# The start of a Fourier-mixing and gated feed-forward kernel, reordered: weight pieces first, then the input in thirds

## The chip, the cores and the metric

One core of a Trainium2 chip runs the whole program. The metric is the device time of one execution in microseconds (us); lower is better. TensorE (PE) multiplies matrices, VectorE (DVE), ScalarE (ACT) and GpSimd (POOL) do elementwise work, SyncE (SP) issues most of the transfers (DMA).

## The reference

```python
x: (8, 3008, 256) float32                       # batch, sequence, features
X = fft(fft(x, axis=1), axis=2).real            # Fourier mixing, real part
t = X.reshape(24064, 256)
gate = 1 / (1 + exp(-(t @ w_gate)))             # w_gate, w_val: (256, 1536)
val  = t @ w_val
out  = (gate * val) @ w_out                     # w_out: (1536, 256)
```

The three weights come as float64, so each stored word is two 32-bit halves, and the kernel makes float32 of them itself.

## The kernel before, in words

**Fourier part.** A sequence of one batch comes as four mirrored rows of slots (x4, 126 partitions, four parts h, six slots q, 256 features). The *fold* adds and subtracts the parts and the mirrored features, so that three kinds of columns are left: cosine columns (0), sine columns (1) and the lone middle feature E (2). PE multiplies them with a table of cosines and sines (`st`, loaded in pieces). The sums of even and odd slots (`ev`, `od`) are left in PSUM, ACT copies the first, DVE adds and subtracts the two (`places`, L509 and L512) into `pk` (cosine rows), `qk` (sine rows) and `ek` (E row). A closure `sums` issues the products of some slots, `then` the evacuation.

**Weights.** The feature transform is merged into the gate and value weights: a *piece* is 256 columns of a weight (512 KB as loaded). Two ACT activations (L297, L298), three DVE operations (L307, L308, L310) and one POOL addition (L312) make float32 of it: `weight_parts` and `weight_join`. `merge` then multiplies a gate or value piece with the table `dt` on PE, ACT copies the product into G1 and G2, and two small DMAs bring the row that belongs to E into `ge`, one column for each tile of features. There are 18 pieces: 6 gate, 6 value, 6 of w_out. A list `jobs` gives their order. For w_out no merge is done; `forms(g)` adds and subtracts its blocks into 15 forms (`wf`) for each of four groups g, on POOL for g = 0 and on DVE for the others.

**Steps.** For each batch the rows are cut into six chunks of 252 and each chunk has 12 tiles of features, so there are 576 steps i. A step has a first half (`front_a`: two products with G1 and pk, for gate and value), a second half (`front_b`: two with G2 and qk), the gates (`gate_a`, `gate_b`, one step later: two sigmoids on ACT, DVE operations z at L640, h at L652 and L654, and sums of h on POOL, L660, none, seven or six of them in three successive steps) and, from step 5 on, a third of `back`: five products that multiply the sums with `wf`, one group of three steps at a time. `back` of group p begins at step 3p + 5, and its first five products need all of `forms` of that group, since the fourth uses form 10, which is made last. The E term is *seeded* into PSUM from step 12 on: ACT writes E times `ge` (L600) before the products are added. In steps 0 to 4 PE adds it by two extra products, in steps 5 to 11 DVE does (L619).

**Order.** The program orders every engine by hand: what is issued first on an engine runs first, and an engine that waits holds all that is issued behind it. `pre` and `use` tell which pieces are converted or used in which step. Transfers on SP also share eight completion semaphores in turn (in the trace), so a later transfer is issued only when the one eight places earlier has landed.

**The start.** Pieces 0 and 1 are loaded, converted and merged, then x (two halves) is folded on DVE and POOL; cosine and E sums run, then the other pieces are converted between the evacuations, the sine sums wait for the second half of the table, and step 0 begins with pieces 2 and 3 still to be merged. The other ten gate and value merges and all forms run between the first steps.

Of the kernel before, what the change touches and what calls it, by code (L numbers as in the profile page):

```python
# [82 lines left out]
def kernel(  # L83
# [61 lines left out]
    def load_x(b):  # L145
        X[b] = xp.tile([P, 4, NQ, D], F32, name="x4", tag="x4")
        for h in range(0, 4, 2):
            if b:
                nc.sync.dma_start(out=X[b][:, h : h + 2], in_=XR[b][:, h : h + 2])
            else:  # L150
                nc.sync.dma_start(out=X[b][0:NP, h : h + 2], in_=xf[b, :, h : h + 2])
# [29 lines left out]
    G1 = const.tile([P, 2, F], F32, name="G1")  # L181
    G2 = const.tile([P, 2, F], F32, name="G2")
# [9 lines left out]
    def load_table(t, nq):  # L192
        for q in range(0, NQ, nq):
            yield nc.sync.dma_start(out=ST[0][0:NP, t, q : q + nq], in_=stab[:, t, q : q + nq])
# [14 lines left out]
    def table_odd():  # L209
# [21 lines left out]
        def tangent():  # L231
# [8 lines left out]
    jobs = [(0, 0), (1, 0), (0, 1), (1, 1), (2, 0), (0, 2), (1, 2), (2, 1), (0, 3), (1, 3), (0, 4), (2, 2),  # L240
            (1, 4), (0, 5), (1, 5), (2, 3), (2, 4), (2, 5)]
    RAW, WS = {}, {}
    shared = {}
    KEEP = 10

    def weight_load(j):
# [13 lines left out]
        def home(j):  # L260

            if j in (0, 1, 2, 3, 5):
                if j > 2:
                    ws = some(5, pqp, "qk")[:, (j // 5) * 2 * WC : (j // 5 + 1) * 2 * WC]
                    return sp.tile([P, 4 * WC], F32, name="raw", tag="sf"), ws
                t = hp.tile([P, 6 * WC], F32, name="raw", tag="h")
                return t[:, 0 : 4 * WC], t[:, 4 * WC :]
            if j in (4, 6, 9):
                t = wf[:, {4: 1, 6: 2, 9: 3}[j]].rearrange("p m n -> p (m n)")
                return t[:, 0 : 4 * WC], t[:, 4 * WC : 6 * WC]  # L270
            t = some(10, cp, "c")
            if j == 7:
                raw = pqp.tile([P, 4 * WC], F32, name="raw", tag="pk")
                return raw, t[:, 6 * WC : 8 * WC]
            return t[:, 0 : 4 * WC], t[:, 4 * WC : 6 * WC]

        if j < KEEP:
            raw, ws = home(j)
        else:
            both = some(24, xp, "x4").rearrange("p (i n) -> p i n", n=2 * WC)  # L280
            r, i = (j - KEEP) % 3 * 2, 6 + (j - KEEP) % 6
            raw, ws = both[:, r : r + 2].rearrange("p a n -> p (a n)"), both[:, i]
# [45 lines left out]

    def merge(ws, g, c, other):
        cs = slice(c * WC, (c + 1) * WC)  # L330
        ps = bank("ps", other)
        for h in range(2):
            for t in range(2):
                mm(ps[:, h * WC : (h + 1) * WC], dt[:, t, h * HD : (h + 1) * HD], ws[:, t, :],
                   h == 0 and t == 0, t == 1)
        nc.scalar.copy(G2[:, g, cs], ps[:, WC : 2 * WC])
        nc.scalar.copy(G1[:, g, cs], ps[:, 0:WC])
        for f in range(c * WC // P, (c + 1) * WC // P):
            (nc.sync if c else nc.scalar).dma_start(
                out=ge[:, g, f : f + 1], in_=G2[0:1, g, f * P : (f + 1) * P])  # L340

# [44 lines left out]
    def fold_ops(b, nq):  # L386
# [51 lines left out]
        else:  # L438

            def half1(q):  # L440
                point(nc.vector, 2, 3, q)
                first(nc.vector, 2, 3, q)
                for blk in range(2):
                    across(nc.vector, blk, q)
                    feat(nc.vector, *parts[blk], q)

            def half2(q):
                across(nc.vector, 0, q)
                feat(nc.vector, *parts[0], q)
                across(pool, 1, q)  # L450
                feat(pool, *parts[1], q)
            for q in qs:
                point(nc.vector, 0, 1, q)
            first(nc.vector, 0, 1, slice(0, NQ))
            point(pool, 2, 3, qs[1])
            first(pool, 2, 3, qs[1])
            ops += [lambda: half1(qs[0]), lambda: half2(qs[1])]
        for blk, (v, r) in enumerate(parts):
            if b and blk:
                W[b, blk] = v[:, :, HD:D], r[:, :, HD:D]  # L460
                continue
            W[b, blk] = (v[:, :, 0:HD], r[:, :, 0:HD],
                         v[:, :, HD : HD + 1].to_broadcast([v.shape[0], NQ, P]))
# [56 lines left out]
    def seq_start(b):  # L520
        PQE[b] = [pqp.tile([P, NK + 1], F32, name=name, tag=name) for name in ("pk", "qk")]
        if not b:
            PQE[b].append(op.tile([P, NK + 1], F32, name="ek", tag="os"))
# [5 lines left out]


# [60 lines left out]
    N1 = 5  # L591

    def seed(i):
# [5 lines left out]
        for g in range(2 if i >= NFT else 0):  # L599
            nc.scalar.activation(PF[i][:, g], EK[i // NFT], AF.Copy, scale=ge[:, g, f : f + 1])  # L600

    def front_a(i):
        (pk, *_), ks, _, _, fs = cut(i)
        if i < NFT:
            seed(i)
        for g in range(2):
            mm(PF[i][:, g], G1[:, g, fs], pk[:, ks], i < NFT and g == 0, True)
        for g in range(2 if i < N1 else 0):
            mm(PF[i][:, g], G2[:, g, fs], shared["qk"][:, 4 * WC : 4 * WC + CH], False, True)

    def part(i):
# [3 lines left out]
        if not N1 <= i < NFT:  # L615
            nc.scalar.activation(AP[i], PF[i], AF.Copy, scale=2.0)  # L616
            return
        for g in range(2):
            nc.vector.scalar_tensor_tensor(out=AP[i][:, g], in0=pqe[2][:, ks],  # L619
                                           scalar=ge[:, g, f : f + 1], in1=PF[i][:, g],  # L620
                                           op0=ALU.mult, op1=ALU.add)
# [6 lines left out]
    def gate_a(i):  # L628
# [7 lines left out]
        if N1 <= i < NFT:  # L636
            nc.vector.scalar_tensor_tensor(out=z[:, :, ::-1], in0=AP.pop(i), scalar=2.0, in1=PF[i],
                                           op0=ALU.mult, op1=ALU.subtract)
        else:
            nc.vector.tensor_tensor(z[:, :, ::-1], AP.pop(i), PF[i], op=ALU.subtract)  # L640
# [6 lines left out]
    def gate_b(i):  # L647
# [5 lines left out]
        nc.scalar.activation(pf[:, 0], z[:, 0], AF.Sigmoid)  # L653
        nc.vector.tensor_tensor(h[:, fh, n:], pf[:, 0], z[:, 1], op=ALU.mult)  # L654
# [145 lines left out]

    nc.gpsimd.memset(nil, 0.0)
# [3 lines left out]
    for j in range(2):  # L805
        weight_load(j)
    load_x(0)
    for _ in load_table(0, NQ // 2):
        pass
    for j in range(2, 5):  # L810
        weight_load(j)
    sines = load_table(1, NQ // 2)
    next(sines)
    for j in range(5, 7):
        weight_load(j)
    next(sines)
    for j in range(7, KEEP):
        weight_load(j)

    def weight_round(*js):  # L820
        for j in js:
            weight_parts(j)
            weight_join(j)

    weight_parts(0)
    weight_parts(1)
    weight_join(0)
    weight_join(1)
    weight_use(0)
    weight_use(1)  # L830
    seq_start(0)

    e0 = shared["qk"][:, 4 * WC : 4 * WC + CH]
    nc.gpsimd.memset(e0, 0.0)
    other = {(0, 0): (4, None), (0, 1): (4, None), (0, 2): (0, 1), (1, 2): (2, 3)}
    cos = [seq_group(0, blk, what, other.get((blk, what))) for blk in range(2) for what in (0, 2)]
    for i, f in enumerate(fold_ops(0, NQ // 2)):
        f()
        for sums, _, _ in cos:
            sums(*range(i * NQ // 2, (i + 1) * NQ // 2))  # L840
    sin = [seq_group(0, blk, 1, other.get((blk, 1))) for blk in range(2)]
    for i in range(2):
        for sums, _, _ in sin:
            sums(*range(i * NQ // 2, (i + 1) * NQ // 2))
    evacuate = [then for _, then, _ in cos + sin]
    for then, js in zip(evacuate, ((2, 3), (4,), (5,), (6,), (7,), (8,))):
        weight_round(*js)
        then()()
    nc.scalar.dma_start(out=ed[0:1], in_=PQE[0][2][0:1])
    nc.vector.tensor_copy(e0[0:1], PQE[0][2][0:1, 0:CH])  # L850
    weight_parts(9)
    for j in range(KEEP, KEEP + 3):
        weight_load(j)
    weight_use(2)
# [8 lines left out]
    pre, use = {}, {}  # L863
    for j, i in enumerate((0, 1, 2, 3, 4, 5, 6, 7, 9), 9):
        if i:
            pre.setdefault(i - 1, []).append(lambda j=j: weight_parts(j))
        pre.setdefault(i, []).insert(0, lambda j=j: weight_join(j))
        if KEEP <= j < len(jobs) - 3:
            at(i, lambda j=j: weight_load(j + 3))
    for j, i in enumerate((0, 0, 1, 2, 0, 3, 4, 5, 4, 6, 7, 8, 8, 8, 11), 3):  # L870
        use.setdefault(i, []).append(lambda j=j: weight_use(j))
    at(N1 - 1, lambda: nc.vector.tensor_copy(PQE[0][1][0:1, 0:CH], PQE[0][2][0:1, 0:CH]))
# [17 lines left out]
    for i in range(i0, count, i0):  # L890
        at(i - 8, lambda i=i: e_rows(i))
# [25 lines left out]
    for i in range(count):  # L917
        front_a(i)
        if N1 <= i < NFT:
            part(i)  # L920
        if i:
            gate_a(i - 1)
        if not N1 <= i < NFT:
            part(i)
        if i0 <= i + 1 < count:
            seed(i + 1)
        if i:
            gate_b(i - 1)
# [67 lines left out]
```

## Time and profile before

| | |
|---|---|
| median of three runs | 1947.45 us (1945.95, 1947.45, 1949.0) |
| the profiled execution's own time | 1951.1 us |
| its span (first to last instruction) | 1949.0 us |
| PE busy | 1917.7 us, 98% of the span |
| POOL, DVE, ACT busy | 1589.7, 1461.0, 1332.5 us |
| granted PE clock, mean of the span | 0.997 |
| loaded and stored by DMA | 97.85 MB, 24.45 MB of it in the first 140 us |

The profile shows one execution: instructions with start and duration, which semaphore ended a wait, and for short stretches the busy time of every engine and the granted clock. Matmuls overlap, so a PE that is busy is not always a PE that gets on at its full pace; the times at which the same product of successive steps starts tell that better. One program product is two MATMUL records, so a `front_b` is four records.

### The profile page before, as it was taken

Reading aid. Unit: us, or ns where it says so; the run is one execution under the profiler, and the core shown is the slowest. Engines: PE = TensorE matmul, PEld = TensorE weight load, DVE = VectorE, ACT = ScalarE, POOL = GpSimd, SP = SyncE. Lnnn points to the kernel's source line nnn. Section 1 sums busy time; section 2 is a strip of 40 time slices with the busy share of each in tenths; the row PEclk is TensorE's granted clock in tenths of the full one; section 3 lists DMA queues with packets and bytes.
Section 4 is the critical chain, followed back from the end, with each engine's and each line's share of the span. In section 5 each row is a group of like instructions: output and inputs, shape, how many; then the busy total and the mean of one; then the engine's idle time right before and its main releaser. Section 6 shows DMA issues by size and latency. Waiting matters only on the chain.

```text
span 1949.0 us, 34556 instructions
## 1 busy us (share of the span) xinstructions
PE 1917.7 (98%) x11262; PEld 1789.8 (92%) x11262; DVE 1461.0 (75%) x3269; ACT 1332.5 (68%) x3125; POOL 1589.7 (82%) x2842
## 2 busy tenths in 40 slices
PE   6999999999999999999999999999999999999999
PEld 3789889999999999999999999999999999999998
DVE  6777787787777777777777777777777777776776
ACT  3567757776777677776777767777677776777775
POOL 3779998997889878987889878888788886777775
PEclk8999999999999999999999999999999999999999
DMA  8352513212012120222012021221210110011101
GB/s 270 90 145 20 118 32 111 47 25 82 14 47 58 17 79 14 57 49 79 14 25 78 18 79 23 45 53 20 82 20 14 19 23 14 14 20 22 25 16 31
DMA packets 168565, 97.85 MB, mean 50 GB/s; under 512 B 131803, under 2 KB 160070, under 8 KB 165838
## 3 DMA queue, kind: packets, MB, share of 16 engines
q1 hardware_dynamic: 167254, 95.12, 20.5%
q8 instruction: 91, 1.49, 0.3%
q14 instruction: 88, 0.72, 0.1%
q10 hardware_dynamic: 1100, 0.51, 0.1%
q0 software_dynamic: 32, 0.00, 0.0%
HBM read 70.35 MB, written 47.24 MB: 60 GB/s over the span
## 4 chain that ended last, share of the span: by engine, by line
PE 92%; DVE 4%; DMA 2%; ACT 1%; issue 0%; SPq 0%; ACTq 0%; DVEq 0%
PE pf L135 48%; PE po L135 40%; PE ev L135 3%; DMA st<-in_stab_dram 1%; DVE c L754 1%; PE od L135 1%; DMA ge<-G 1%; PE ps L135 1%; DVE z L640 1%; ACT pf L653 0%; DVE h L654 0%; DVE h L652 0%; PE row L135 0%; DVE wf L375 0%; DMA raw<-in_moe_w_val_dram 0%
## 5 line engine op out<-in xcount | busy, mean ns | idle before, releaser
L660 POOL TENSOR_TENSOR sf<-h 128x168 f32<-128x168 f32 (+1 forms) x955 | 530.8, 574 | 225.1 <-DVE h L654 225.0
L660 POOL TENSOR_TENSOR sf<-h,sf 128x168 f32<-128x168 f32 (+1 forms) x1146 | 638.4, 576 | 61.5 <-DVE h L654 60.9
L135 PE MATMUL pf<-qk,G 128*128 128x252 f32 (+1 forms) x2304 | 583.2, 376 | 4.2 <-DVE ae L619 2.3
L135 PE MATMUL pf<-pk,G 128*128 128x252 f32 (+1 forms) x2304 | 583.5, 376 | 1.6 <-DVE h L654 1.4
L654 DVE TENSOR_TENSOR h<-pf,z 128x252 f32<-128x252 f32 (+1 forms) x576 | 241.5, 419 | 420.0 <-ACT pf L653 420.0
L600 ACT ACTIVATE pf<-ek,ge 128x252 f32<-128x252 f32 (+1 forms) x1128 | 531.4, 471 | 18.7 <-DVE h L654 0.2
L135 PE MATMUL po<-sf,wf 128*128 128x168 f32 (+1 forms) x3056 | 527.5, 305 | 0.0
L616 ACT ACTIVATE ae<-pf 128x504 f32<-128x504 f32 (+1 forms) x569 | 335.0, 589 | 233.8 <-PE pf L135 232.5
L135 PEld LDWEIGHTS pf<-pk,G 128*128 128x128 f32 x2304 | 436.1, 190 | 55.7 <-DVE h L654 3.2
L135 PEld LDWEIGHTS po<-sf,wf 128*128 128x128 f32 x3056 | 470.4, 190 | 8.2
L135 PE MATMUL po<-h,wf 128*128 128x168 f32 (+1 forms) x2674 | 473.9, 306 | 0.2 <-DVE wf L372 0.2
L754 DVE TENSOR_TENSOR c<-c 128x168 f32<-128x168 f32 (+1 forms) x949 | 450.6, 506 | 5.2
L135 PEld LDWEIGHTS po<-h,wf 128*128 128x128 f32 x2674 | 425.5, 190 | 17.2 <-DVE wf L372 0.6
L135 PEld LDWEIGHTS pf<-qk,G 128*128 128x128 f32 x2304 | 409.9, 190 | 31.6 <-ACT ae L616 3.1
L640 DVE TENSOR_TENSOR z<-ae,pf 128x504 f32<-128x504 f32 (+1 forms) x569 | 378.4, 665 | 25.0 <-ACT h L635 23.4
L635 ACT ACTIVATE h<-pf 128x252 f32<-128x252 f32 (+1 forms) x576 | 217.7, 378 | 155.5 <-PE pf L135 147.8
L653 ACT ACTIVATE pf<-z 128x252 f32<-128x252 f32 (+1 forms) x576 | 214.4, 372 | 113.7 <-DVE h L652 111.1
L652 DVE TENSOR_TENSOR h<-h,pf 128x252 f32<-128x252 f32 (+1 forms) x576 | 232.3, 403 | 0.0
L660 POOL TENSOR_TENSOR sf<-sf 128x168 f32<-128x168 f32 (+1 forms) x191 | 109.5, 573 | 15.0
L660 POOL TENSOR_TENSOR sf<-sf,h 128x168 f32<-128x168 f32 (+1 forms) x191 | 104.2, 545 | 0.0
L135 PE MATMUL ev<-st,x 63*128 63x189 f32 (+3 forms) x372 | 73.1, 347 | 9.4 <-DVE x L403 6.6
L688 ACT COPY c<-po 128x504 f32<-128x504 f32 (+1 forms) x144 | 81.7, 568 | 0.0
(148 smaller groups left out, 888.8 us busy)
## 6 DMA issues: line engine op xcount, KB each, us to landing
x<-xr SPq DMA_DIRECT2D x14, 1536.0 KB
out_dram<-os SPq DMA_DIRECT2D x376, 56.0 KB
xr<-in_xf_dram SPq DMA_DIRECT2D x14, 768.0 KB
xr<-in_xf_dram SPq DMA_DIRECT2D x35, 256.0 KB
ek<-ed SPq DMA_DIRECT2D x39, 126.0 KB
out_dram<-os SPq DMA_DIRECT2D x288, 7.0 KB
st<-in_stab_dram SPq DMA_DIRECT2D x4, 1111.9 KB
x<-in_xf_dram SPq DMA_DIRECT2D x2, 1512.0 KB
```

The source lines that it names most:

```text
L135: nc.tensor.matmul(o, l, r, start=start, stop=stop, skip_group_check=True)
L600: nc.scalar.activation(PF[i][:, g], EK[i // NFT], AF.Copy, scale=ge[:, g, f : f + 1])
L616: nc.scalar.activation(AP[i], PF[i], AF.Copy, scale=2.0)
L635: nc.scalar.activation(H[p][:, fh, 0:n], PF[i][:, 0], AF.Sigmoid)
L640: nc.vector.tensor_tensor(z[:, :, ::-1], AP.pop(i), PF[i], op=ALU.subtract)
L652: nc.vector.tensor_tensor(h[:, fh, 0:n], h[:, fh, 0:n], pf[:, 1], op=ALU.mult)
L653: nc.scalar.activation(pf[:, 0], z[:, 0], AF.Sigmoid)
L654: nc.vector.tensor_tensor(h[:, fh, n:], pf[:, 0], z[:, 1], op=ALU.mult)
L660: nc.gpsimd.tensor_tensor(block(p, dst), block(p, a), block(p, b), op=(ALU.subtract, ALU.add)[op])
L688: (nc.vector.tensor_copy if t == 1 or t == 3 and not last else nc.scalar.copy)(C[0][:, 3 * t * R : 3 * (t + 1) * R], PO[t][:, 0 : 3 * R])
L754: engine.tensor_tensor(t[:, dst * R : (dst + 1) * R], *v, op=(ALU.subtract, ALU.add)[op])
```

## The change

Order of the pieces: the first eight are now gate and value pieces of four column ranges. All eight are loaded first, converted one after the other, and merged, with the ACT copy of a merge issued three pieces later and as one instruction for both halves. 14 products on a tile of ones are issued on PE ahead of them. Then x comes in three slices of two slots (128 partitions), each followed by its cosine table (in two DMAs of 112 and 14 partitions); each slice is folded on DVE alone. E is multiplied as a single column, its four sums (even, odd, two blocks) at partitions 0, 32, 64 and 96 of one bank. E's first 252 values are spread over partitions by one product with ones, so ACT can seed from step 0; the extra products and the DVE additions of E are gone. The `ge` DMAs of the eight pieces, 16 of them, are issued on SP after the x and cosine loads and ahead of the sine tables. The sine sums are issued in thirds with the first halves of steps 0, 1 and 2 between them. Pieces 8 and 9 are converted after that and piece 10 begun; 10 to 17 are converted inside steps 0 to 9, between the two DVE operations of `gate_b`. The E row of a chunk is loaded three steps earlier.

```diff
+    def load_third(j):
+        q = slice(2 * j, 2 * j + 2)
+        rows = xf.rearrange("b p h q d -> (b p) h q d")
+        nc.sync.dma_start(out=X[0][:, :, q], in_=rows[0:P, :, q])
...
+    def load_table(t, j):
+        q = slice(2 * j, 2 * j + 2)
+        for rows in (slice(0, 112), slice(112, NP)):
+            nc.sync.dma_start(out=ST[0][rows, t, q], in_=stab[rows, t, q])
...
-    jobs = [(0, 0), (1, 0), (0, 1), (1, 1), (2, 0), (0, 2), (1, 2), (2, 1), (0, 3), (1, 3), (0, 4), (2, 2),
-            (1, 4), (0, 5), (1, 5), (2, 3), (2, 4), (2, 5)]
+    jobs = [(0, 0), (1, 0), (0, 1), (1, 1), (0, 2), (1, 2), (0, 3), (1, 3), (0, 4), (1, 4), (2, 0), (2, 1),
+            (0, 5), (1, 5), (2, 2), (2, 3), (2, 4), (2, 5)]
...
+    def merged(j):
+        g, c = jobs[j]
+        ps = MERGED.pop((g, c))
+        cs = slice(c * WC, (c + 1) * WC)
+        nc.scalar.copy(G[:, :, g, cs], ps.rearrange("p (h n) -> p h n", h=2))
+
+    def ge_load(j):
+        g, c = jobs[j]
         for f in range(c * WC // P, (c + 1) * WC // P):
-            (nc.sync if c else nc.scalar).dma_start(
-                out=ge[:, g, f : f + 1], in_=G2[0:1, g, f * P : (f + 1) * P])
+            nc.sync.dma_start(out=ge[:, g, f : f + 1], in_=G2[0:1, g, f * P : (f + 1) * P])
...
+            tt = nc.vector.tensor_tensor
+            def third(q):
+                a, m = x4[:, 0:3:2, q], x4[:, 1:4:2, q]
+                tt(a[:, :, :, 0], a[:, :, :, 0], m[:, :, :, 0], op=ALU.add)
+                tt(a[:, :, :, 1:D], a[:, :, :, 1:D], m[:, :, :, D - 1 : 0 : -1], op=ALU.add)
+                across(nc.vector, 0, q)
+                across(nc.vector, 1, q)
+            def feats(q):
+                v, r = x4[:, 0:2, q], x4[:, 2:4, q]
+                nc.vector.memset(r[:, :, :, 0:1], 0.0)
+                lo, hi = v[:, :, :, 1:HD], v[:, :, :, D - 1 : HD : -1]
+                tt(r[:, :, :, 1:HD], lo, hi, op=ALU.subtract)
+                tt(lo, lo, hi, op=ALU.add)
...
+    def e0_sums(j):
+        if not j:
+            E0["ps"] = bank("pe", NB - 1)
+        for q in (2 * j, 2 * j + 1):
+            for blk in range(2):
+                c0, n = ((0, NE), (NE, NO))[blk]
+                row = (2 * blk + q % 2) * TB
+                mm(E0["ps"][row : row + 1, 0:n], W[0, blk][2][:, q], ST[0][0:NP, 0, q, c0 : c0 + n],
+                   not j, j == N3 - 1)
+
+    def e0_copies():
...
+        for i in range(4):
+            nc.scalar.copy(a[i], ps[i * TB : i * TB + 1, 0 : a[i].shape[1]])
+
+    def e0_row():
...
+        places(er, 0, True, od, ev)
+        places(er, 1, False, ev1, od1)
+
+    def e0_spread():
+        ps = bank("ek", NB - 1)[:, 0:CH]
+        mm(ps, busy[0:1, 0:P], shared["er"][:, 0:CH], True, True)
+        EK[0] = ekp.tile([P, CH], F32, name="ek", tag="ek")
+        nc.scalar.copy(EK[0], ps)
...
-        for g in range(2 if i >= NFT else 0):
+        for g in range(2):
             nc.scalar.activation(PF[i][:, g], EK[i // NFT], AF.Copy, scale=ge[:, g, f : f + 1])
...
-        for g in range(2 if i < N1 else 0):
-            mm(PF[i][:, g], G2[:, g, fs], shared["qk"][:, 4 * WC : 4 * WC + CH], False, True)
...
-        for g in range(2):
-            nc.vector.scalar_tensor_tensor(out=AP[i][:, g], in0=pqe[2][:, ks],
-                                           scalar=ge[:, g, f : f + 1], in1=PF[i][:, g],
-                                           op0=ALU.mult, op1=ALU.add)
+        nc.scalar.activation(AP[i], PF[i], AF.Copy, scale=2.0)
...
+    def gate_b(i, between=()):
         nc.vector.tensor_tensor(h[:, fh, 0:n], h[:, fh, 0:n], pf[:, 1], op=ALU.mult)
         nc.scalar.activation(pf[:, 0], z[:, 0], AF.Sigmoid)
+        for f in between:
+            f()
         nc.vector.tensor_tensor(h[:, fh, n:], pf[:, 0], z[:, 1], op=ALU.mult)
...
+    warm(14)
+    for j in range(8):
+        weight_parts(j)
+        if j > 2:
+            merged(j - 3)
+        weight_join(j)
+        weight_use(j)
+    for j in range(5, 8):
+        merged(j)
+    for j in range(8):
+        ge_load(j)
+    for j in range(N3):
+        load_table(1, j)
+    for j in range(8, KEEP):
+        weight_load(j)
...
+    for j in range(N3):
+        folds[2 * j]()
+        e0_sums(j)
+        folds[2 * j + 1]()
+        if j == N3 - 1:
+            e0_copies()
+            e0_row()
+        for sums, _, _ in cos:
+            sums(2 * j, 2 * j + 1)
+    put = [then() for _, then, _ in cos]
+    for f in put:
+        f()
+    e0_spread()
...
+    sines(0)
+    first(0)
+    sines(1)
+    first(1)
+    sines(2)
+    first(2)
+    for _, then, _ in sin:
+        then()()
...
+    for j in (8, 9):
+        weight_parts(j)
+        weight_join(j)
+    weight_parts(10)
...
+    for j, i in ((8, -2), (9, -1), (10, 0), (11, 1), (12, 2), (13, 3), (14, 4), (15, 6), (16, 7), (17, 9)):
+        if i > 0:
             pre.setdefault(i - 1, []).append(lambda j=j: weight_parts(j))
+        if i >= 0:
+            mid.setdefault(i, []).append(lambda j=j: weight_join(j))
+        use.setdefault(i + 1 + (jobs[j][0] < 2), []).append(lambda j=j: using(j))
...
-        at(i - 8, lambda i=i: e_rows(i))
+        at(i - 11, lambda i=i: e_rows(i))
```

## The prediction

> **What bounds the kernel now.** First the page's busy times, then the timelines of PE, DVE, POOL and SP over the first 130 us.
>
> ```profile
> PE 1917.7 (98%) x11262; PEld 1789.8 (92%) x11262; DVE 1461.0 (75%) x3269; ACT 1332.5 (68%) x3125; POOL 1589.7 (82%) x2842
> ```
>
> PE is busy 98% of the span, so outside the start nothing but PE counts. From PE's timeline, what the sums below use:
>
> ```profile
> 45.48 1.63 PE L135 MATMUL ev<-st,x 126*128 126x377 f32 x2 [2.78 <-DMA st<-in_stab_dram]
> 46.90 2.42 PE L135 MATMUL od<-st,x 126*128 126x377 f32 x4
> ...
> 56.27 1.01 PE L135 MATMUL pf<-qk,G 128*128 128x252 f32 x4
> ...
> 79.42 1.59 PE L135 MATMUL po<-h,wf 128*128 128x168 f32 x10
> 80.90 1.12 PE L135 MATMUL pf<-qk,G 128*128 128x252 f32 x4
> ...
> 110.94 1.12 PE L135 MATMUL pf<-qk,G 128*128 128x252 f32 x4
> ...
> 120.88 1.01 PE L135 MATMUL pf<-qk,G 128*128 128x252 f32 x4
> 124.01 1.01 PE L135 MATMUL pf<-qk,G 128*128 128x252 f32 x4
> ```
>
> These are the second halves of steps 0 (56.27), 5 (80.90), 11 (110.94), 14 and 15. From 14 to 15 it takes 3.13 us, which is PE's own work (0.85 first half, 0.85 second, 1.43 back). Steps 5 to 11 take 5.0 us each. Behind step 14 PE hardly waits, so the change is worth what it moves step 14's second half from 120.88: everything behind it shifts by the same.
>
> What holds the early steps is DVE: in 60 to 120 us its timeline has hardly an idle stretch but the half microsecond before each L654, and the work there is gates (z 0.59, two h of 0.34 from start to start), joins of pieces 9 to 17, forms, and the E additions (L619, 0.77 a step).
>
> **Change, part by part.** (a) *Eight pieces first.* Two neighbouring joins, from the timeline of the stretch:
>
> ```profile
> 29.80 0.69 DVE L310 SCALAR_TENSOR_TENSOR raw<-raw 128x512 int32<-128x512 int32 x1
> 30.41 0.42 DVE L307 TENSOR_SCALAR wqk<-wqk 128x512 f32<-128x512 f32 x1
> 30.63 1.34 POOL L312 TENSOR_TENSOR raw<-raw 128x512 int32<-128x512 int32 x1 [1.14 <-DVE raw L310]
> 30.86 1.40 DVE L308 TENSOR_SCALAR wqk<-wqk 128x512 int32<-128x512 int32 x1
> 32.29 0.69 DVE L310 SCALAR_TENSOR_TENSOR wqk<-raw,wqk 128x512 int32<-128x512 int32 x1
> ```
>
> L308 alone takes 0.43; here it lasts until 0.29 behind POOL's addition. So a piece costs 32.29 - 29.80 = 2.49 us in a row of pieces, more than ACT (two activations at 0.57 and a copy of 0.59: 1.73) or loading (512 KB at 0.37 MB/us of the stretch 5 to 10: 1.4). Before, piece 1's L310 ends at 10.11; six more end at 25.05, the last POOL addition at 26.5, its merge (1.73) at 28.3.
>
> (b) *Fold.* L393 with 765 elements takes 0.91 from start to start, L401 with 381 some 0.53: 1.2 for 1020, 0.62 for 512. A third is 0.1 + 1.2 + 2 x 0.62, and 0.1 + 2 x 0.62 for its features: 3.9. Three end at 36.8. The six pieces that now go ahead of x are 3.1 MB, 9.5 us of loading at 0.33 MB/us (the mean rate of 5 to 30 us, with 0.85 MB at 5). x's last slice (9.1 MB with all before it) lands at 30, needed at 32.9, the last cosines (9.9 MB) at 32.4, needed at 35.5. The joins hide this with 3 us to spare; without that cover, lateness is paid one to one.
>
> (c) *E in column tiles.* The batch sums of E later in this kernel have the same form, with 7 columns:
>
> ```profile
> L135 PE MATMUL pe<-st,x x24: 477/479/490, 203.3 to 204.9; 126*7 126x377 f32 x12, 126*7 126x376 f32 x12
> ```
>
> 24 records in 2.1 us, against 24 x 0.315 = 7.6 in a row: 0.7 a third. With the cosine sums (8 records, 2.5) PE needs 3.2 a third and waits for DVE; the cosine sums end at 36.8 + 2.5 = 39.35. E's four copies (0.46, L557; ACT) and four additions (0.47, DVE) end at 39.1, pk's four at 41.1.
>
> (d) *Sine sums and first halves*: three thirds of 2.5 and three halves of 0.85. The first third waits for banks that DVE frees at 40.1 and 41.1, and ends at 42.4; the rest follows without a gap: 49.1, and 49.95 with the third half. qk is done at 50.4, against 52.88 before (L512 at 52.34, 0.54). The sine tables, and behind them pieces 8 to 13, now queue on SP behind 16 `ge` DMAs, of which the last eight (0.55 us each to issue) follow the last cosines: issued from 36.8, the three pairs land at about 40.5, 43 and 45; needed at 40, 43.3 and 46.6. I take 0 and keep 1 for the range.
>
> (e) *Piece 8* is converted only behind qk: join 1.61, POOL 1.3, so its merge starts at 53.5 and PE is idle for 3.5 us. After 2.78 idle us PE ran at half pace above (four records in 2.42 instead of 1.43), so the merge takes 3.4: step 0's second half starts at 56.9, later than 56.27. Steps 1 and 2 have no first half to do.
>
> (f) *Steps 1 to 5: POOL.* Before, two thirds of forms(0) were done by 59.5; now all of it stands in POOL's queue between the sums of h and the additions:
>
> ```profile
> 64.74 2.87 POOL L660 TENSOR_TENSOR sf<-h 128x168 f32<-128x168 f32 x4
> ...
> 69.06 1.33 POOL L372 TENSOR_TENSOR wf<-wf 128x256 f32<-128x256 f32 x2
> 70.36 1.46 POOL L312 TENSOR_TENSOR wx<-wx 128x512 int32<-128x512 int32 x1
> ```
>
> The joins inside the gates put L654 of step 1 at 63.6 (gate 0 with join: 0.59 + 0.34 + 1.61 + 0.34 from 57.8; join 12 waits until POOL has added piece 11). From 63.3: three additions at 1.3, seven sums at 0.6, six at 0.52, forms 1.5 + 1.5 + 1.2 = 15.4, so forms(0) ends at 78.7. The fourth product of back(0) waits for it on PE, and front_b(5) stands behind; PE has been idle for most of 70 to 78.7, so its last two products and the half (0.57 + 0.85) take double: 81.6, against 81.75 before. Up to here nothing is won.
>
> (g) *Steps 6 to 14.* Left on DVE to the end of forms(2): three gates with a join at 3.4 (2.1 a join beside a busy POOL, as L307 to L310 from 65.14), two without at 1.7, five parts of forms at 1.0: 18.5, so back(2) starts at 100.1 and step 11's second half at 101.5, against 110.94. Gone from DVE in these steps are six E additions (0.8), one join (2.3) and three of the half-microsecond waits before L654, which joins now fill: 8.6 of the 9.3 won here. ACT takes over the seeds (0.98 for two): 2.3 us a step, 4 with the activations of a piece, within the 3.4 to 5 of these steps except where it waits with PE for POOL. Then PE's own 3.13: step 14 at 110.9. 120.88 - 110.9 = 10.0 us. The E rows, issued three steps earlier, find the buffer free (its last seed is three steps back) and are read 11 steps later; the products on ones run while PE waits for piece 0 (8.70): 0 for both, and a late row would hold the seeds of its chunk.
>
> Bounds of what no row shows: join pace 2.2 to 2.89 (POOL's end 8.64 to 11.53 for the two first pieces), -2 to +3; PE full pace at (e) and (f), -1.7 and -1.4; sums of h at 0.5 or 0.71, -1.5 to +3; sine tables at 0.24 MB/us (30 to 45) instead of 0.33, 2.6 later on top of the 1: +3.5. I take the middle rows, since each is the case nearest in engine mix.
>
> **A page against the trace.** For the pace of (a) the row is 2.49, with L307 slipped in beside POOL. Ahead of eight joins in a row a rule speaks against the change: the Trainium skill, SBUF — State Buffer, "Who interferes with whom", says VectorE and GpSimd share a port pair as an exclusive lock: whoever starts second is blocked to the end. The trace agrees on L308, which lasts to POOL's end, and not on L307, which ends inside POOL's 1.34. By the row the sum is -10.0, by the rule -6.8.
>
> **Rivals.**
> *No slip*: every piece takes 2.89, as pieces 0 and 1 did. That is 0.4 on eight pieces: -6.8 us. Against: the 2.49 row. Chance 0.12. This is what that page's lock would make of it.
> *Columns do not overlap* (the change does not do what it says): E costs 2.5 a third, PE 5.0 against DVE's 3.9: cosine sums 2.6 later, -7.4. Against: the 24 records. 0.03.
> *POOL is no wall*: sums at 0.5 (-1.5) and full pace of PE at (e) and (f) (-3.1), where the waits fall outside whatever slows it: -14.6. For it: POOL's sums alone take 0.52. Against: the row after 2.78 idle us. 0.15.
> *POOL is a wall in every step*: sums at 0.71 and additions at 1.51 (3.02 for two at 75.60): 13 x 0.71 + 2.25 = 11.5 per three steps against DVE's 9.3. +3.2 at (f), twice 2.2 behind: -2.4. For it: 3.02 for two additions; against: seven additions at 1.3 elsewhere. 0.08.
> *Slower: the sine tables stuck behind `ge`.* SP waited 10.7 us, before two later loads, for the halves of x to land and give up their semaphores (the waits of SP):
>
> ```profile
> SPq L290 <- DMA x<-in_xf_dram: 10.7, 2, 5.5
> ```
>
> In the chain of waits one `ge` copy took 10.55 us to land, a later one 1.75:
>
> ```profile
> 16.35 10.55 DMA ge<-G
> ...
> 84.20 1.75 DMA ge<-G
> ```
>
> The last sine piece takes the semaphore that x's last slice frees at 30, by way of two `ge` copies. If each of the three takes 10.55, it lands at 30 + 3 x 10.55 = 61.7 instead of 46.6: +15.1, so +5.1 and 1952.6. It turns slower once the lateness is over 10. For it: the copies are issued into full queues. Against: the second eight find the queues nearly empty, as the one of 1.75 did. 0.12.
>
> **Numbers.** The sum is made against the profiled execution (1951.1, span 1949.0), 3.65 over the median; a shift in us holds for both. Forecast, chance 0.50: 1947.45 - 10.0 = 1937.5, its own range -6 to -13. Rivals: 1940.7, 1940.1, 1932.9, 1945.1, 1952.6. The range 1930.5 to 1946 leaves out the slower rival and a little of the fastest. What can be told from no change is 0.2%, 3.9 us. Faster: 0.50 + 0.12 + 0.03 + 0.15 = 0.80, less 0.02 for a forecast that falls short by over 6, 0.78; same: 0.08 and that 0.02, 0.10; slower 0.12.
>
> **What would show it.** L310 of piece 7 at 25, fold's end at 37, cosine sums' end at 39.4, qk at 50.4, second half of step 0 at 57, a PE wait of some 5 us for forms(0) on POOL before the second half of step 5 at 80, back(2) at 100, step 14 at 111. Wrong if piece pace, sine tables or POOL's queue miss these by over 3 us, or if steps behind 14 no longer take 3.13.

## The result, and the profile after

| | before | after |
|---|---|---|
| median | 1946.88 us (20 runs, 1945.02 to 1949.92) | 1952.80 us (20 runs, 1950.02 to 1955.74) |
| ratio | | 1.003, 95% interval 1.0023 to 1.0037 |
| the profiled execution: time, span, granted clock | 1951.1, 1949.0, 0.997 | 1954.44, 1952.7, 0.993 |

The change costs 5.9 us; forecast was a gain of 10. The ratios, here and below, are taken over the runs of both kernels and need not equal the quotient of the medians: runs of before scatter by up to 14 us (1945.41 to 1959.66 beside e5 to e8). In the profiled pair the difference is smaller, 3.3 us in time: the profiled execution of before is slower than all 20 runs of the table.

The page's busy times of after: PE is at 98% again, the question is the start alone.

```profile
PE 1923.0 (98%) x11272; PEld 1792.9 (92%) x11272; DVE 1456.7 (75%) x3258; ACT 1347.9 (69%) x3147; POOL 1582.1 (81%) x2835
```

VectorE's timeline of after, the last operation of two neighbouring joins: start, duration, engine, line. The pieces come every 2.49 us, as forecast.

```profile
21.60 0.69 DVE L315 SCALAR_TENSOR_TENSOR wf<-wf 128x512 int32<-128x512 int32 x1
24.08 0.69 DVE L315 SCALAR_TENSOR_TENSOR wf<-wf 128x512 int32<-128x512 int32 x1
```

PE's timeline of after; in brackets the wait ahead and what ended it:

```profile
40.85 0.69 PE L135 MATMUL ek<-er,busy 1*128 1x252 f32 x2
44.88 1.60 PE L135 MATMUL ev<-st,x 126*128 126x377 f32 x2 [3.34 <-DMA st<-in_stab_dram]
46.27 1.46 PE L135 MATMUL od<-st,x 126*128 126x377 f32 x2
...
61.43 3.78 PE L135 MATMUL ps<-wf,dt 128*128 128x256 f32 x8 [3.53 <-POOL wf L317]
65.00 1.89 PE L135 MATMUL pf<-qk,G 128*128 128x252 f32 x4
...
75.11 2.05 PE L135 MATMUL pf<-qk,G 128*128 128x252 f32 x4 [2.16 <-ACT ae L657]
...
87.17 0.55 PE L135 MATMUL po<-h,wf 128*128 128x168 f32 x2 [1.52 <-POOL wf L386]
89.55 0.84 PE L135 MATMUL po<-h,wf 128*128 128x168 f32 x4 [1.82 <-POOL wf L386]
90.22 1.01 PE L135 MATMUL pf<-qk,G 128*128 128x252 f32 x4
...
102.32 1.49 PE L135 MATMUL po<-h,wf 128*128 128x168 f32 x4 [3.13 <-DVE wf L386]
...
124.64 1.01 PE L135 MATMUL pf<-qk,G 128*128 128x252 f32 x4
```

Three things are to be seen. The first sine sums wait 3.34 us for their table, where the forecast had no wait. Behind that wait, and behind those at 61.43, 75.11 and 102.32, PE runs at half pace: two records of a sine sum take 1.46 instead of 0.80, four of a second half 1.89 or 2.05 instead of 1.01. And step 14 comes at 124.64, not 110.9. The windows of after show the half pace as granted clock (the number behind the busy times), and what the transfers do beside it (their busy share, then GB/s):

```profile
40.00:50.00 10.00, 6.66 (x13) 3.34 (x13) 2.44 (x6) 1.87 (x5) 0.00 (x0) 0.67 0.99 245
50.00:60.00 10.00, 7.90 (x29) 5.20 (x27) 3.48 (x8) 6.81 (x14) 0.00 (x0) 0.99 0.97 338
60.00:70.00 10.00, 8.57 (x27) 7.12 (x28) 7.33 (x12) 4.26 (x9) 3.92 (x3) 0.66 0.46 171
```

In the same windows before, the clock was 0.83, 1.00 and 1.00. Why the table is late stands in the chain of waits of after (start, duration, link): a cosine table holds a semaphore for 17.93 us, a row of `ge` copies follows at 0.47 to 0.61 us each, and only then the first sine table is issued, at 39.14; it needs 4.97 us to land.

```profile
14.83 17.93 DMA st<-in_stab_dram
...
32.82 0.47 SPq L354
...
38.49 0.60 SPq L354
...
39.14 0.59 SPq L199
...
39.77 4.97 DMA st<-in_stab_dram
```

### The profile page after: what moved, and what is told of

Its sections match the earlier page's. It is cut to its first block, busy times and chain, and to the rows that moved or that the text cites. A ratio compares the mean times of both kernels' runs of the same rounds, so it can differ in the third digit from the quotient of the medians.

```text
span 1952.7 us, 34586 instructions
## 1 busy us (share of the span) xinstructions
PE 1923.0 (98%) x11272; PEld 1792.9 (92%) x11272; DVE 1456.7 (75%) x3258; ACT 1347.9 (69%) x3147; POOL 1582.1 (81%) x2835
## 4 chain that ended last, share of the span: by engine, by line
PE 93%; DVE 3%; DMA 2%; POOL 1%; ACT 1%; SPq 1%; issue 0%; ACTq 0%; DVEq 0%; POOLq 0%
PE pf L135 48%; PE po L135 40%; PE ev L135 3%; DMA st<-in_stab_dram 1%; PE od L135 1%; DVE c L788 1%; DMA wf<-in_moe_w_val_dram 1%; DVE z L672 0%; POOL sf L694 0%; PE row L135 0%; ACT pf L685 0%; SPq L354 0%; DVE h L688 0%; DVE h L684 0%; POOL wf L386 0%
## 5 line engine op out<-in xcount | busy, mean ns | idle before, releaser
L646 ACT ACTIVATE pf<-ek,ge 128x252 f32<-128x252 f32 (+1 forms) x1152 | 542.8, 471 | 20.0 <-DVE h L688 1.1
L657 ACT ACTIVATE ae<-pf 128x504 f32<-128x504 f32 (+1 forms) x576 | 339.1, 589 | 244.3 <-PE pf L135 241.8
L672 DVE TENSOR_TENSOR z<-ae,pf 128x504 f32<-128x504 f32 (+1 forms) x576 | 383.5, 666 | 27.4 <-ACT h L671 25.8
L135 PE MATMUL ev<-st,x 63*128 63x189 f32 (+3 forms) x360 | 68.8, 341 | 4.5 <-DMA st<-in_stab_dram 3.3
```

The lines of the kernel that those rows point to most:

```text
L135: nc.tensor.matmul(o, l, r, start=start, stop=stop, skip_group_check=True)
```

## The experiments

All are edits of the kernel after unless said otherwise. Second halves (`front_b`) of four steps, from PE's timelines in us, and the median beside the kernel before of the same group of runs:

| run | step 0 | step 5 | step 8 | step 14 | median | over before of its group | ratio (95%) |
|---|---|---|---|---|---|---|---|
| before | 56.27 | 80.90 | 98.68 | 120.88 | 1946.9 | | |
| after | 65.00 | 90.22 | 103.60 | 124.64 | 1952.8 | +5.9 | 1.0030 (1.0023 to 1.0037) |
| e1 | 60.98 | 86.16 | 99.53 | 120.53 | 1949.8 | +2.2 | 1.0004 (0.9993 to 1.0015) |
| e2 | 65.52 | 89.83 | 102.60 | 123.27 | 1951.6 | +4.0 | 1.0013 (1.0001 to 1.0025) |
| e3 | 65.82 | 90.75 | 104.01 | 124.70 | 1953.6 | +6.0 | 1.0030 (1.0021 to 1.0039) |
| e4 | 64.83 | 85.47 | 99.58 | 120.56 | 1949.9 | +2.3 | 1.0011 (1.0001 to 1.0020) |
| e5 | 60.99 | 85.97 | 99.23 | 119.89 | 1949.6 | +2.1 | 0.9997 (0.9984 to 1.0009) |
| e6 | 59.26 | 84.26 | 98.13 | 118.23 | 1950.1 | +2.6 | 1.0011 (1.0002 to 1.0020) |
| e7 | 57.64 | 82.58 | 96.47 | 117.67 | 1946.1 | -1.4 | 0.9990 (0.9981 to 1.0000) |
| e8 | 56.34 | 75.65 | 91.08 | 111.18 | 1943.1 | -4.4 | 0.9966 (0.9951 to 0.9981) |
| e9 | 63.41 | 84.81 | 99.00 | 119.90 | 1950.5 | +5.1 | 1.0027 (1.0016 to 1.0038) |
| e10 | 58.61 | 78.82 | 92.57 | 112.18 | 1940.2 | -5.2 | 0.9971 (0.9960 to 0.9983) |
| e11 | 56.87 | 77.13 | 94.33 | 115.29 | 1945.4 | 0.0 | 1.0000 (0.9991 to 1.0009) |
| e12 | 56.53 | 75.83 | 90.66 | 111.32 | 1943.1 | -2.3 | 0.9988 (0.9979 to 0.9996) |
| e13 (after again) | 62.26 | 87.45 | 100.83 | 122.02 | 1952.1 | +6.5 | 1.0038 (1.0026 to 1.0051) |
| e15 | 60.55 | 81.86 | 96.13 | 116.95 | 1949.8 | +4.2 | 1.0019 (1.0009 to 1.0029) |
| e14 | 54.69 | 74.91 | 88.67 | 108.27 | 1938.5 | -7.1 | 0.9964 (0.9952 to 0.9977) |

The groups are e1 to e4, e5 to e8, e9 to e12, and e13 to e15. The kernel before ran about 2 us faster in the last two (1945.4 and 1945.6, against 1947.6 and 1947.5), which were measured on other chips, so times of different groups are compared by the column "over before" only.

The steps come from one execution each. The kernels after, e9, e13 and e15 are the same up to step 0, and their second halves of step 0 stand at 65.00, 63.41, 62.26 and 60.55. So 4 us at step 0 alone prove nothing between two such traces; differences between steps repeat better (steps 0 to 5 take 25.2 us in after and in e13).

**e1: sine tables first.** Theory A: the tables' place in SP's queue is the cause. Theory B: POOL's queue sets the end.

```diff
-    for j in range(8):
-        ge_load(j)
     for j in range(N3):
         load_table(1, j)
+    for j in range(8):
+        ge_load(j)
```

> The six sine table loads go ahead of the 16 ge copies in SP's queue; nothing else moves. Theory A (the tables' place in SP's queue is the cause): PE's wait of 3.34 us before the first sine half falls under 0.5 us, the first sine third takes 2.5 us instead of 5.1 us (no half clock behind the wait), the last qk write ends near 52.5 us instead of 58.4, all that follows shifts by 5.9 us, and the time is about 1947 us, level with before. Theory B (POOL's queue at steps 2 to 6, busy without a break from 73.6 to 93 us, sets the end): qk comes early as in A, but front_b(5) still comes near 88 to 90 us and the time stays at 1951 to 1953 us. Theory C (what is lost is half clock after whichever wait stands there): half of A's shift, 1949 to 1950 us.

The wait ahead of the sine sums is gone and the last qk write ends at 52.63, as A said. But step 0's second half gains 4.0 us, not 5.9, and the time is theory C's. SP's and PE's timelines of e1:

```profile
33.03 16.03 SPq L354 DMA_DIRECT2D ge<-G  x16
49.11 0.59 SPq L295 DMA_DIRECT2D wf<-in_moe_w_gate_dram  x1
```

```profile
57.40 3.78 PE L135 MATMUL ps<-wf,dt 128*128 128x256 f32 x8 [5.23 <-POOL wf L317]
```

The 16 copies now wait for the sine tables' semaphores, and piece 8 is issued behind them at 49.11 instead of 42.05: the wait moved from the tables to piece 8 (5.23 instead of 3.53 us, half pace behind it as before).

**e2: pieces 8 and 9 converted between the sine thirds**, and **e3: this and e1's order.**

```diff
         seed(i)
+        weight_parts(8 + i)
+        if i < 2:
+            weight_join(8 + i)
         front_a(i)
...
-    for j in (8, 9):
-        weight_parts(j)
-        weight_join(j)
-    weight_parts(10)
```

> The tables stay behind the ge copies; pieces 8 and 9 are converted (and the parts of piece 10 made) between the sine thirds, where DVE and POOL stand idle, instead of behind the qk writes. Theory A: qk unchanged near 58.4 us, or up to 1 us later where ScalarE waits for piece 8; PE's wait of 3.53 us before piece 8's merge and the half clock behind it (1.9 us) go, step 0's second half at about 60 instead of 65.0 us, time about 1947.5 us. Theory B: that gain is given back before 90 us, time 1951 to 1953 us.

> Both edits of the two kernels before it. Theory A: the two waits lie one behind the other, so both gains add: step 0's second half near 54.5 us, front_b(5) near 80 us, time about 1942 us, under before by 0.25%. Theory B: the chain on POOL takes it back, 1949 to 1952 us.

Step 0's second half comes no sooner in either, so theory A is out in both; e2's 1951.6 us lies in theory B's range, but not by B's mechanism, since there was no gain to give back, and e3's 1953.6 lies outside both. ScalarE takes its work in order, and now stands at piece 8 ahead of the seeds of step 1. PE's timeline of e3:

```profile
56.87 2.05 PE L135 MATMUL pf<-pk,G 128*128 128x252 f32 x4 [8.17 <-ACT pf L646]
```

Piece 8 was issued at 49.87 there. So an early conversion is worth nothing while the piece is late, and a wait of 5.2 us became one of 8.2. That gave the theory called C from e6 on: not the tables, but whatever load stands behind the 16 copies is late.

**e4: e3, and the first third's form sums on VectorE.**

```diff
-        engine = nc.vector if g else nc.gpsimd
+        engine = nc.vector
```

> As the kernel before it, and the form sums of the first third of the output matrix (L386, 5.1 us on POOL) are issued to VectorE, so that POOL's queue holds only the joins' additions and the H sums there. Theory A: no more than 1 us from the kernel before it, about 1941 to 1943 us. Theory B: here the time falls, by 4 us or more below the kernel before it, since the POOL waits of 1.52 and 1.82 us ahead of front_b(5) and the 3.13 us ahead of front_b(8) go.

Step 0 as in e3 (64.83), but step 5 comes 4.3 us sooner against step 0, and the time falls by 3.7 us, a little under B's 4: B is right on the two waits ahead of front_b(5), which go. The one ahead of front_b(8) does not; it is 3.86 us, against 1.32 in e3.

**e5: half clock.** Products of no use in the two long waits of the kernel after.

```diff
     e0_spread()
+    warm(7)
...
+        if j == 8:
+            warm(8)
         weight_use(j, 1 + j % 3)
```

> The kernel after, with 7 products of no use (252 columns of ones into a spare bank) put into TensorE's wait for the first sine table and 8 into its wait for piece 8; no wait is shortened. If the half clock behind the two waits is part of the price, the first sine third takes 2.5 instead of 5.1 us and piece 8's merge 1.9 instead of 3.8 us, step 0's second half comes 4.5 to 5 us sooner, at about 60 us, and the time is about 1948 us. If the length of the waits alone counts, or what follows gives it back (POOL's chain), the time stays at 1952 to 1953 us.

PE's timeline of e5:

```profile
42.23 3.24 PE L135 MATMUL warm<-busy 128*128 128x252 f32 x14 [0.46 <-ACT ek L576]
...
60.99 1.01 PE L135 MATMUL pf<-qk,G 128*128 128x252 f32 x4
```

The transfers and conversions are where they were, and step 0's second half comes 4.0 us sooner than in after; step 14 keeps 4.75. Beside e5's full pace, the first sine third and the merge of piece 8 take 4.4 us longer in after, but 2.1, 2.1 and 0.7 us longer in e9, e13 and e15, which have the same start. So the half clock behind the two waits is about 4 of the 8.7 us by which step 0 is later than before in this trace of after, and less in others. In time, e5 is 2.1 us over before where after is 5.9, and the intervals of the two ratios lie apart.

**e6: SP's order, e7: with e2's conversion, e8: with e4's forms.**

```diff
-    for j in range(8):
-        ge_load(j)
     for j in range(N3):
         load_table(1, j)
-    for j in range(8, KEEP):
+    weight_load(8)
+    for j in range(2):
+        ge_load(j)
+    for j in range(9, KEEP):
         weight_load(j)
+        ge_load(j - 7)
+    ge_load(7)
```

> SP's order is sine tables, piece 8, then the 16 ge copies in pairs between the loads of pieces 9 to 13; no engine's work is reordered. Theory C (loads wait in SP's queue behind the 16 copies, and in the first run the wait only moved from the tables to piece 8, issued at 49.1 us there): both come in time; no wait before the sine thirds, qk written at about 52.5 us, piece 8 landed by 46 us, its merge held only by its own conversion (3.5 us behind the last first half), at about 56 instead of 57.4 us of the first run or 61.4 us of the kernel after; time about 1947.5 to 1948.5 us. Theory B (POOL's chain at steps 2 to 6): 1950 us or more.

> That order, and pieces 8 and 9 (and the parts of 10) converted between the sine thirds. Theory C: now the loads are there when ScalarE comes to them, PE has no wait from 41 us to step 0's second half, which comes at about 54.5 us, 10 us sooner than in the kernel after; front_b(5) at about 80 us; time about 1942 to 1943 us. Theory B: POOL takes it back at steps 3 to 6, 1948 us or more.

> As the kernel before it, with the first third's form sums on VectorE. Among the kernels of the first call this edit was worth 3.7 us (1953.6 to 1949.9). Theory C, with what POOL was seen to take: 3 to 4 us less than the kernel before it, about 1939 us, under before by 0.4%. If the edit only helped there because half clock fell elsewhere: no more than 1 us.

In e6 the profiled execution took 1948.1 us, as C said, but the median is 1950.1, which is B's number; steps 0 to 5 take 25.0 us as in after (25.2), so the early start was not given back there and step 14 comes 6.4 us sooner. e7 shows C's main point: with piece 8 there in time, the same conversion that cost 3.8 us beside e1's order gains 4.0 beside this one. Step 0 comes at 57.64, not 54.5: PE still waits 1.74 us for the seed and 1.74 us for the bank of piece 8, and the time lies between C's and B's. e8 takes off 3.0 us more, within C's 3 to 4, and is the first kernel clearly under before: from step 0 to 5 it needs 19.3 instead of 24.9 us.

**e10: e8 with piece 8 merged in a spare bank and every later piece one step sooner.**

```diff
-        weight_use(j, 1 + j % 3)
+        weight_use(j, 1 + j % 3 if j > 8 else 4)
...
-    for j, i in ((8, -2), (9, -1), (10, 0), (11, 1), (12, 2), (13, 3), ...
+    for j, i in ((8, -2), (9, -1), (10, -1), (11, 0), (12, 1), (13, 2), ...
```

> The best kernel so far (SP's order, early conversion, forms on VectorE; 1943.1 us) with piece 8's merge in the spare bank, so that it needn't wait for the qk writes (PE's wait of 1.72 us at 54.5 us), piece 10 joined and piece 11's parts made before the qk writes, and all later pieces one step sooner. If waits before step 3 still reach the end: 2.5 to 4 us less, about 1940 us. If the form sums of the second third on VectorE (a wait of 4.2 us at 89.8 us) now set the end: within 1 us of 1943 us.

Over before it is 0.8 us better than e8, with intervals that overlap: not told apart. Step 0 even came later, since the first seed did. The chain of waits of e10:

```profile
34.81 10.90 DMA ge<-G
```

One `ge` copy, half a KB, took 10.9 us to land behind the sine tables and piece 8. (The chain of before had one of 10.55.)

**e11: e8 with the second third's forms on POOL, e12: e8 with 3 and 5 products of no use at step 3.**

```diff
-        engine = nc.vector
+        engine = nc.gpsimd if g == 1 else nc.vector
```

> The 1943.1 us kernel with the second third's form sums on POOL instead of VectorE, the first third's on VectorE. If VectorE's load is what makes the wait of 4.21 us ahead of the products of step 8: the wait falls to under 2 us and the time to 1941 us. If the form sums are late because their pieces of the output matrix are (joined at steps 4 and 6), the engine does not matter: the wait stays at 3 to 5 us, and the time within 1 us of 1943 us, or worse by POOL's H sums.

> The 1943.1 us kernel with 3 and 5 products of no use in TensorE's waits of 1.51 and 2.19 us at step 3 (62.3 and 65.6 us), where the granted clock of 60 to 70 us is 0.83. If the waits of step 3 cost half clock as well: the clock there is 1.00, and the time falls by 1 to 1.7 us, to 1941.5 us; if they are too short to matter, or if the 4.21 us wait behind them takes it back: 1943 us or more.

PE's timelines of e11 and of e12, and e12's window of step 3:

```profile
90.22 0.93 PE L135 MATMUL po<-h,wf 128*128 128x168 f32 x2 [4.40 <-POOL wf L386]
93.05 1.49 PE L135 MATMUL po<-h,wf 128*128 128x168 f32 x4 [1.90 <-POOL wf L386]
```

```profile
89.98 0.84 PE L135 MATMUL po<-h,wf 128*128 128x168 f32 x4 [4.20 <-DVE wf L386]
```

```profile
60.00:70.00 10.00, 9.40 (x42) 7.32 (x41) 9.15 (x18) 8.87 (x23) 7.04 (x9) 1.00 0.09 18
```

e11: the other engine makes it worse, 2.7 us between steps 0 and 8; the forms of the second third are late on either. e12: the clock in 60 to 70 us is 1.00 instead of e8's 0.83, and step 4's second half comes 1.0 us sooner (69.80 against 70.78), but step 5's does not (75.83 against 75.65), the products of step 8 wait until 89.98 instead of 89.80, and the span is 1939.4 instead of 1939.3. In these two traces half clock ahead of waits that end at the same time cost nothing. The medians add no gain either: over before, e12 is 2.3 us faster and e8 in its group 4.4.

**e9, e13, e15: the forms alone.** e9 and e15 are the kernel after with e4's line only; e13 is the kernel after, run beside e15.

> The kernel after with one edit: the first third's form sums (5.1 us on POOL) go to VectorE. The edit was worth 3.7 us in the first call and 3.0 us in the second, on other orders. If POOL's queue is a price of its own (the waits of 1.52 and 1.82 us ahead of front_b(5)), independent of the tables: about 3 us, 1949.5 us, and front_b(5) comes 3 to 5 us sooner than at 90.2 us. If it matters only once the start is early: no more than 1 us, 1952 us or more.

> The form sums alone on VectorE, beside the kernel after on the same chip. Theory P (POOL's queue is a price of its own in the kernel after): 2.5 to 4 us under the kernel after. Theory Q (the forms' move only pays once the pieces come early, since otherwise the wait for the second third's forms, 3.9 us instead of 3.1 us, takes its place): within 1 us of the kernel after.

e9 came to 1950.45 us, 5.1 over before (ratio 1.0027, 1.0016 to 1.0038), which alone could not be told from the kernel after. Beside it, e15 is 2.3 us under e13. Steps 0 to 5 take 21.3 instead of 25.2 us (21.4 in e9); steps 5 to 8 give back 0.9, where the wait for the second third's forms is 4.03 instead of 3.13 us. PE's timeline of e15:

```profile
94.85 1.49 PE L135 MATMUL po<-h,wf 128*128 128x168 f32 x4 [4.03 <-DVE wf L386]
```

From step 0 to step 14 it is 56.4 us (56.5 in e9) instead of 59.8 (59.6 in after), so the traces are theory P's and Q's full replacement is out. The size in time stays open: 2.3 us lies under P's range, e9 over before is only 0.8 us better than after, and the intervals overlap.

**e14: e10 with the four `ge` copies of pieces 0 and 1 ahead of the sine tables.**

```diff
+    for j in range(2):
+        ge_load(j)
     for j in range(N3):
         load_table(1, j)
     weight_load(8)
-    for j in range(2):
-        ge_load(j)
```

> The 1940.2 us kernel with the 4 ge copies of pieces 0 and 1 issued ahead of the sine tables. There one of these copies took 10.9 us to land behind the big loads, ScalarE's first seed waited for it until 45.8 us, and TensorE waited 2.30 us with half clock behind (the first seed's products 2.05 instead of 1.12 us). If the order of that queue still sets the start: that wait and its half clock go, 3 to 4 us sooner at step 0, and if steps 1 to 9 (paced by the conversions on VectorE and ScalarE) do not take it back, 1937 us; if they do, 1939 to 1940.5 us.

PE's timeline of e14, step 0 and the longest waits of the start, and a window that had half clock in after:

```profile
54.69 1.12 PE L135 MATMUL pf<-qk,G 128*128 128x252 f32 x4 [0.80 <-DVE qk L520]
...
61.73 1.12 PE L135 MATMUL pf<-pk,G 128*128 128x252 f32 x4 [2.50 <-ACT pf L646]
...
88.67 1.12 PE L135 MATMUL pf<-qk,G 128*128 128x252 f32 x4 [2.51 <-ACT ae L657]
```

```profile
40.00:50.00 10.00, 10.00 (x35) 5.99 (x34) 5.73 (x12) 6.80 (x15) 1.30 (x1) 1.00 0.95 266
```

Step 0 comes 3.9 us sooner than in e10, and step 14 keeps it. The median, 1938.5, lies between the two numbers expected; over before it is 1.9 us better than e10, with intervals that overlap, so the two are not told apart in time. It beats both kernels: 0.9964 of before (0.9952 to 0.9977), and 13.6 us under e13. Its five runs lie within 1.1 us of one another at mean clocks of 0.997 to 1.000, against 3.9 us at 0.994 to 0.996 for the five of e13.

## Why the prediction was wrong, point by point

*(a) right.* 2.49 us a piece, the last L315 done at 24.77 (25.05 forecast). The rival "no slip" is out: a piece takes 2.49 and not 2.89. On the page about the lock: L313 lasts 1.39 us, as the Trainium skill, SBUF — State Buffer, "Who interferes with whom" would have it. The 2.89 was not that rule's, though, since by it the second to start is blocked, and in the row of pieces L312 starts ahead of the addition (22.20 against 22.42). Between pieces 0 and 1 VectorE waits 0.63 us for ScalarE, L312 starts behind the addition (7.54 against 7.05) and lasts 1.09 us, and the piece takes 2.91.

*(b), (c) right but for 1.3 us.* The column sums of E take 0.81 us a third (0.7 forecast); "columns do not overlap" is out. The fold ends at 38.07 instead of 36.8, the first third being 1.2 longer, and pk is done at 42.4 instead of 41.1.

*(d) is the step that failed.* It let the tables' path cost nothing. It let eight copies follow the last cosines and the tables land at 0.33 MB/us. In the trace ten copies stand behind a cosine table that gives up its semaphore at 32.76, and take 6.3 us to issue; the first sine table goes out at 39.14 (36.8 forecast) and lands at 44.74 (40.5), and the queues are full at only 245 GB/s, the slow end of my bounds. The first sine third starts 5.0 us late, at 44.88; 3.3 of this is the wait for the table, most of the rest the later fold of (b). It then takes 5.1 instead of 2.5 us at half clock: qk is done at 58.37 instead of 50.4. The wait and the half clock together, 5.9 us, are what e1 takes back at qk (52.63). The rival with the tables stuck behind the copies named this mechanism and was given 0.12; its price, 15.1 us at the tables, was too high, but half clock and the later steps made up for it, so its 1952.6 lies 0.2 us from the median by sizes that are not its own. e1, e6 and e7 show that the queue is the cause: the lateness goes where the order of the loads sends it. It is not all of the loss: e6, which changes the queue alone, gets back 3.3 of the 5.9 us in time and, in its trace, 6.4 of the 13.7 us by which step 14 missed the forecast.

*(e) right, but shifted.* The wait for piece 8 is 3.53 us (3.5) and its merge 3.78 (3.4). Both start 8 us later. The 3.78 is this trace's; behind the same wait the merge took 2.46 to 2.63 us in e9, e13 and e15. What it missed: DVE and POOL have nothing to do from 42.4 to 56.4, so this cost need not be there at all; e7 and e14 take it away.

*(f) mis-sized by 2.3 us.* The chain that ends with forms(0) in POOL's timeline of after, its first and last operation:

```profile
73.61 1.28 POOL L317 TENSOR_TENSOR wc<-wc 128x512 int32<-128x512 int32 x1 [2.25 <-ACT wqk L303]
...
88.99 0.51 POOL L386 TENSOR_TENSOR wf<-wc,wf 128x128 f32<-128x128 f32 x1
```

forms(0) ends at 89.5 instead of 78.7, of which 8.1 are the late start; 2.3 of the other 2.7 reach step 5, which comes 25.2 us behind step 0 instead of 22.9 (78.7 and the two doubled products give 79.8). The chain itself takes 15.9 us, near the 15.4 taken, with seven sums of h at 0.62 each (0.6). It starts 8.6 us behind step 0 instead of 6.4, mostly as the first gate starts 2.4 us behind it instead of 0.9. That forms(0) stands in POOL's queue is a price of its own: 3.9 us by step 5 and 3.4 by step 14 (e15 against e13), 2.3 in the medians. "POOL is no wall" is out by its sums and by (e); that PE goes on at full pace behind forms(0) it had right. "POOL is a wall in every step" is out too: POOL stands idle for 1.5 to 1.6 us three times between 93 and 109.

*(g) mis-sized by 3.4 us.* Steps 5 to 11 take 25.0 us instead of 21.7 (79.8 to 101.5). The sum ran to the end of forms(2) and gave forms(1) no wait. The trace has the 3.13 us wait at 102.32 for forms(1) on VectorE, whose parts take 2.1 to 2.4 us instead of the 1.0 I took, and half clock behind it (from 102.32 to the next second half at 109.01 it takes 6.7 us, where four records of `back`, two halves and ten records at full pace are 0.57 + 2 x 0.85 + 1.43 = 3.7). The second part of forms(1) in VectorE's timeline of after:

```profile
94.86 1.46 DVE L386 TENSOR_TENSOR wf<-wx,wf 128x256 f32<-128x256 f32 x1
96.24 0.76 DVE L386 TENSOR_TENSOR wf<-wf,wx 128x256 f32<-128x256 f32 x1
```

Moving forms(1) to POOL (e11) does not help. What remains open is what order of pieces and forms would remove that wait; e14 has waits of 2.5 us for ScalarE there instead.

The end of the sum, too: from step 14 on the steps take 3.13 us as forecast, and step 14's shift of 3.8 us is the span's (3.7). The 8.1 us at step 0, 2.3 of (f) and 3.4 of (g) make up the 13.7 by which step 14 missed. The change of the medians, 5.9, missed by 15.9, 2.2 us more: the sum was made against an execution of before 4.2 us over its median, that of after is 1.6 over its own, so a shift in us did not hold for both; no trace shows where the faster executions of before gain. Between steps 0 and 14 the change does win, 5.0 us (64.6 to 59.6), where 10.6 were forecast; but step 0 comes 8.7 us later than before, where 0.6 were forecast.

## What to carry to other kernels

Where transfers are issued in order and share a few semaphores, list them in issue order with what each waits for; many tiny copies ahead of a needed load cost their issue time and the waits of all semaphores in between. A wait moved out of one place comes up at the next load in the queue, so change the order of the whole queue and look again before converting or computing anything earlier. Price a wait of TensorE with the half clock behind it as a range (here 0.7 to 4.4 us for the same two waits), and only where nothing behind that wait ends later anyway. Read a start from more than one execution.

## What was not expected of the hardware

TensorE's clock fell after shorter waits than thought. The Trainium skill, TensorE: Matmul & The Clock Gate, "Why this matters for your kernels", warns of idle gaps over about 3 us. Here waits of 3.34 and 3.53 us agree, but one of 2.16 us, behind another of 1.27 us 3 us earlier, also gave half pace (75.11 of after: four records in 2.05 us). And the length alone does not decide: 2.92 us ahead of the first sine sums gave half pace in e13 (two records in 1.59 us), 2.74 us in e15 did not (0.87 us). The merge of piece 8 shows it best, in order in e13, e15 and e6: behind waits of the same length it takes 3.78 us in after, 2.46 and 2.63 here, and in e6 it runs at full pace.

```profile
60.01 2.46 PE L135 MATMUL ps<-wf,dt 128*128 128x256 f32 x8 [3.53 <-POOL wf L317]
...
58.13 2.63 PE L135 MATMUL ps<-wf,dt 128*128 128x256 f32 x8 [3.53 <-POOL wf L317]
...
57.43 1.99 PE L135 MATMUL ps<-wf,dt 128*128 128x256 f32 x8 [3.54 <-POOL wf L317]
```

The 20 runs of after differ by 5.7 us; half clock that falls differently is a likely part of it, but no run shows how much.

A copy of half a KB can take 10.9 us to land when it is issued behind large loads (e10), and there ScalarE's first seed waited for it; with the first copies issued 14 us sooner PE has no such wait (e14).
